# The first column group of x0: from a transposing load to two row loads and TensorE transposes

## The chip, the cores and the metric

The kernel runs on one core of one Trainium2 chip. The metric is the device time of one execution in microseconds (us); lower is better. Before the change it is 133.1 us, the median of three runs (133.09, 133.1 and 134.2).

The engines are named as in the profile: PE is TensorE (PEld its weight loads), DVE is VectorE, ACT is ScalarE, POOL is GpSimd, SP is SyncE. SPq and ACTq are the DMA queues that SP and ACT issue on.

## The reference

Six cross layers over a batch of 4096 rows with 416 features, all in bfloat16:

```python
B, F, D, L = 4096, 26, 16, 6
Din = min(F * D, 1024)          # 416
# x0: (B, Din), ws: (L, Din, Din), bs: (L, Din), all bfloat16
x = x0
for l in range(L):
    x = x0 * (x @ ws[l] + bs[l]) + x
return x
```

## The kernel before

**Layout.** In the first five layers x is held transposed: features on the partitions, batch rows along the columns. The 416 features are three blocks of 128 (the tiles `XM`, one column block k for each) and a remainder of 32 (the tiles `XR`). The batch is cut into two super-blocks s of 2048 columns, each into four groups g0 to g3 of 512. `XM[0]` holds x0 transposed. The remainder of the four groups of one s is stacked on the 128 partitions of `XR[0]`; `XRd` holds the same with the halves swapped. `ident` is an identity matrix for transposes on PE.

**Loads.** `load_x0t(s, g)` (L74) brings 512 rows of x0, the first 384 features, transposed by the DMA into `XM[0]`: 384 KiB each, eight of them, all issued by SP. `load_wm(eng, l)` (L71) brings the main rows of layer l's weights (312 KiB), `load_wr0` (L87) the last 32 rows of layer 0's weights, four times, into `WR`. `load_xrem0` (L78) brings the remainder of x0 for s = 0 in four pieces of 64-byte segments into `xrig`, `load_xrem1` (L83) that of s = 1. `bsb` gets the biases. The order of the issues is the order of the program on each queue (L99 to L120): on SP the transposing loads of s = 0's g0 to g3, s = 1's g0, `xrem`, s = 1's g1 to g3, then the weights of later layers; on ACT the weights of layer 0, the biases, the four pieces of `xrig`, `WR`, and then one activation (L105), ahead of which the activation table is loaded. In this text T0 to T7 are the eight transposing loads in the order in which SP issues them, and WM0 and WR0 are the loads of layer 0's weights.

**PE before the data.** `pe_filler(8)` (L130) runs eight matmuls on constants. `bias_setup` (L137) transposes the biases on PE, and DVE copies them to `bM` and `bR`.

**First layer.** `first_layer(s)` (L197) takes two groups at a time (h = 0: g0, g1; h = 1: g2, g3). `full(m, gl)` (L202) accumulates three matmuls (k = 0 to 2) for output block m of one group. For s = 0, h = 0 the order is all of g0, then `x0_rem(0, ...)` (L146), which transposes the four pieces of `xrig` on PE and has DVE copy them to `XR[0]` and `XRd`, then all of g1. After that come the matmuls over the remainder rows (L223), which need `WR`, `XR[0]` and `XRd`. Then h = 1 does the same with g2 and g3, in the order m outer, group inner, and the matmuls of the remainder outputs (`mm_rem`). `ew_main` (L153) is the rest of a layer for one output block: ACT adds the bias out of PSUM, DVE multiplies by x0 and adds x.

**PSUM.** One pool of four buffers, each of two banks, serves all tiles of PE's output in turn (`tag="ps"`); a tile waits until the buffer that it takes is free.

**Afterwards.** Layers 1 to 4 are loops over (s, m) with PE, ACT and DVE overlapped; the last layer computes rows again and stores them.

Of the kernel before, what the change touches and what calls it, by code (L numbers as in the profile page):

```python
# [9 lines left out]
ACT = mybir.ActivationFunctionType  # L10
ALU = mybir.AluOpType
BF16 = mybir.dt.bfloat16
FP32 = mybir.dt.float32
# [3 lines left out]
def kernel(  # L17
# [7 lines left out]
    nc = tc.nc  # L25
    B, D = x0.shape
    L = ws.shape[0]
    P = 128
    NK = 3
    R = D - NK * P  # L30
    assert R == 32 and B == 4096 and D == 416 and L >= 2
    NS = 2
    NG = 4
    CW = 512
# [5 lines left out]
    big = ctx.enter_context(tc.tile_pool(name="big", bufs=1))  # L40
    tpool = ctx.enter_context(tc.tile_pool(name="tpool", bufs=4))
    opool = ctx.enter_context(tc.tile_pool(name="opool", bufs=10))
    psum = ctx.enter_context(tc.tile_pool(name="psum", bufs=4, space=bass.MemoryType.PSUM))

    x0_v = x0.rearrange("(bt p) d -> p bt d", p=P)
    out_v = out.rearrange("(bt p) d -> p bt d", p=P)

    ident = const.tile([P, P], BF16)
    dz = const.tile([P, 2], FP32)
    warm = const.tile([P, CW], BF16)  # L50
# [6 lines left out]
    bM = const.tile([P, NK, L], FP32)  # L57
    bR = const.tile([P, L], FP32)
    X0rows = big.tile([P, NBT, D], BF16)
    XLrows = big.tile([P, NBT, D], BF16)  # L60
    scrR = [big.tile([P, 4, P], BF16, name=f"scrR{s}") for s in range(NS)]
    xrem = big.tile([P, 16, R], BF16)
    xrig = big.tile([P, NS, 4, P], BF16)
    XRd = big.tile([P, NS * CW], BF16)
    XM = [big.tile([P, NK, B], BF16, name=f"XM{i}") for i in range(3)]
    XR = [big.tile([P, NS * CW], BF16, name=f"XR{i}") for i in range(3)]

    def col0(s, g):
        return SW * s + CW * g

    def load_wm(eng, l):  # L71
        eng.dma_start(WM[:, l], ws[l, 0:NK * P, :].rearrange("(k p) n -> p k n", p=P))

    def load_x0t(s, g):  # L74
        c0 = col0(s, g)
        nc.sync.dma_start_transpose(out=XM[0][:, :, c0:c0 + CW], in_=x0[c0:c0 + CW, 0:NK * P])  # L76

    def load_xrem0():  # L78
        with nc.allow_non_contiguous_dma(reason="64B row segments"):
            for i in range(4):  # L80
                nc.scalar.dma_start(xrig[:, 0, i, :].rearrange("p (g r) -> p g r", g=NG), x0_v[:, i:16:4, NK * P:D])

    def load_xrem1():  # L83
        with nc.allow_non_contiguous_dma(reason="64B row segments"):
# [2 lines left out]
    def load_wr0():  # L87
        nc.scalar.dma_start(WR[:, 0, :], ws[0:1, NK * P:D, :].broadcast_to([NG, R, D]))
# [7 lines left out]
    nc.gpsimd.memset(ones[:], 1.0)  # L96
    nc.gpsimd.memset(WD[:], 0.0)

    load_x0t(0, 0)  # L99
    load_wm(nc.scalar, 0)  # L100
    nc.scalar.dma_start(bsb[:], bs[:, :])
    load_x0t(0, 1)
    load_xrem0()
    load_wr0()
    nc.scalar.activation(dz[:, 1:2], dz[:, 0:1], ACT.Identity, bias=dz[:, 0:1], scale=1.0)  # L105
    for g in range(2, NG):
        load_x0t(0, g)
    load_x0t(1, 0)
# [13 lines left out]
    def fill_wd(l0, l1):  # L122
        for g in range(NG):
            nc.gpsimd.tensor_copy(WD[32 * g:32 * g + 32, l0:l1, g, :], WR[32 * g:32 * g + 32, l0:l1, NK * P:D])  # L124

    fill_wd(0, 1)
    nc.gpsimd.tensor_copy(xrig[:, 1].rearrange("p i (g r) -> p i g r", g=NG), xrem[:].rearrange("p (g i) r -> p i g r", g=NG))
    fill_wd(1, L)

    def pe_filler(n):  # L130
        wps = psum.tile([P, CW], FP32, tag="ps", name="wps")
        for i in range(n):
            nc.tensor.matmul(wps[:], lhsT=warm[:, 0:P], rhs=warm[:], start=(i == 0), stop=(i == n - 1))  # L133

    pe_filler(8)

    def bias_setup():  # L137
        pb = psum.tile([P, 4, 8], BF16, tag="ps", name="pb")
        for m in range(NK):
            nc.tensor.transpose(pb[:, m, 0:L], bsb[0:L, 128 * m:128 * m + 128], ident[0:L, 0:L])  # L140
        for g in range(NG):
            nc.tensor.transpose(pb[32 * g:32 * g + 32, 3, 0:L], bsb[0:L, NK * P:D], ident[0:L, 0:L], tile_position=(0, 32 * g))
        nc.vector.tensor_copy(bM[:], pb[:, 0:NK, 0:L])
        nc.vector.tensor_copy(bR[:], pb[:, 3, 0:L])

    def x0_rem(s, tpr):  # L146
        for i in range(4):
            nc.tensor.transpose(tpr[:, 128 * i:128 * i + 128], xrig[:, s, i, :], ident[:])
        for dst, src in ((slice(0, P), slice(0, P)), (slice(64, P), slice(0, 64)), (slice(0, 64), slice(64, P))):
            to = XR[0] if dst == src else XRd  # L150
            nc.vector.tensor_copy(to[dst, CW * s:CW * s + CW], tpr[src])

    def ew_main(l, s, m, h, pt, cur, nxt):  # L153
        c0 = col0(s, 2 * h)
        t = tpool.tile([P, 2 * CW], BF16, name="t")
        nc.scalar.activation(t[:], pt[:].rearrange("p a b -> p (a b)"), ACT.Identity, bias=bM[:, m, l:l + 1], scale=1.0)  # L156
        nc.vector.tensor_tensor(out=t[:], in0=t[:], in1=XM[0][:, m, c0:c0 + 2 * CW], op=ALU.mult)  # L157
        nc.vector.tensor_tensor(out=nxt[:, m, c0:c0 + 2 * CW], in0=t[:], in1=cur[:, m, c0:c0 + 2 * CW], op=ALU.add)  # L158

    def ew_rem(l, s, pr, curR, nxtR):  # L160
        tr = tpool.tile([P, 2 * CW], BF16, name="t")
        nc.scalar.activation(tr[:, 0:CW], pr, ACT.Identity, bias=bR[:, l:l + 1], scale=1.0)  # L162
        nc.vector.tensor_tensor(out=tr[:, 0:CW], in0=tr[:, 0:CW], in1=XR[0][:, CW * s:CW * s + CW], op=ALU.mult)
        nc.vector.tensor_tensor(out=nxtR[:, CW * s:CW * s + CW], in0=tr[:, 0:CW], in1=curR[:, CW * s:CW * s + CW], op=ALU.add)  # L164
# [15 lines left out]
    def mm_rem(l, s, pr, cur, curR):  # L180
        for g in range(NG):
            nc.tensor.matmul(pr[32 * g:32 * g + 32, :], lhsT=WD[:, l, g, :], rhs=curR[:, CW * s:CW * s + CW],  # L182
                             start=True, stop=False, tile_position=(0, 32 * g))
        for k in range(NK):
            for g in range(NG):
                c0 = col0(s, g)
                nc.tensor.matmul(pr[32 * g:32 * g + 32, :], lhsT=WM[:, l, k, NK * P:D], rhs=cur[:, k, c0:c0 + CW],  # L187
                      start=False, stop=(k == NK - 1), tile_position=(0, 32 * g))
# [8 lines left out]
    def first_layer(s):  # L197
        cur, curR, nxt, nxtR = XM[0], XR[0], XM[1], XR[1]
        for h in range(2):
            pt = [psum.tile([P, 2, CW], FP32, tag="ps", name=f"ph{m}") for m in range(NK)]  # L200

            def full(m, gl):  # L202
                c0 = col0(s, 2 * h + gl)
                for k in range(NK):
                    nc.tensor.matmul(pt[m][:, gl, :], lhsT=WM[:, 0, k, 128 * m:128 * m + 128], rhs=cur[:, k, c0:c0 + CW],  # L205
                                     start=(k == 0), stop=False)

            if s == 0 and h == 0:
                for gl in range(2):
                    for m in range(NK):  # L210
                        full(m, gl)
                    if gl == 0:
                        tp0 = psum.tile([P, CW], BF16, tag="ps", name="tpr")
                        x0_rem(0, tp0[:])
            else:
                for m in range(NK):
                    for gl in range(2):
                        full(m, gl)
            for m in range(NK):
                for gl in range(2):  # L220
                    rg = 32 * ((2 * h + gl) ^ (2 if m == 1 else 0))
                    src = XRd if m == 1 else curR
                    nc.tensor.matmul(pt[m][:, gl, :], lhsT=WR[rg:rg + 32, 0, 128 * m:128 * m + 128],  # L223
                                     rhs=src[rg:rg + 32, CW * s:CW * s + CW],
                                     start=False, stop=True, tile_position=(rg, 0))
            if h == 1:
                pr = psum.tile([P, 2, CW], FP32, tag="ps", name="pr")
                mm_rem(0, s, pr[:, 0, :], cur, curR)
                if s == 0:
                    x0_rem(1, pr[:, 1, :].bitcast(BF16)[:, 0:CW])  # L230
            for m in range(NK):
                ew_main(0, s, m, h, pt[m], cur, nxt)
            if h == 1:
                ew_rem(0, s, pr[:, 0, :], curR, nxtR)

    bias_setup()
    for s in range(NS):
        first_layer(s)

# [41 lines left out]
    l = LL  # L281
# [98 lines left out]
```

## Time and profile before

| what | us |
|---|---|
| median of three runs | 133.1 |
| the profiled execution, own time | 133.1 |
| its span, first to last instruction | 131.2 |
| PE busy | 122.8 (94%) |
| DVE busy | 108.2 (83%) |
| ACT busy | 83.0 (63%) |
| POOL busy | 7.6 (6%) |
| the eight transposing loads, issue to landing, least / median / most | 4.8 / 5.6 / 6.5 |

The mean granted clock of TensorE is 0.998 of full speed. A busy PE is not a PE at its peak: matmuls are pipelined, and one of 512 columns is listed with 0.38 us while the next starts earlier. The DMA share of a core is the mean over its 16 DMA engines.

```profile
L76 SPq DMA_TRANSPOSE XM<-in_x_dram x8: 1378/2044/2574, 0.7 to 16.1; - x8
DMA to landing us min/median/max: 4.8/5.6/6.5
```

These two lines are from the instructions that touch the tile XM: SP spends 1.4 to 2.6 us on the issue of each transposing load (the numbers are ns, least, median and most, then the first and last start in us), and each lands 4.8 to 6.5 us after its issue began.

### The profile page before, as it was taken

The numbers are of one execution on the slowest core, as the hardware profiler recorded it, in microseconds if no ns is written. First come the engines' busy times: TensorE is split into PE (matmuls) and PEld (weight loads), VectorE is DVE, ScalarE is ACT, GpSimd is POOL, SyncE is SP. The second block draws the span as 40 slices with busy tenths as digits, with TensorE's granted clock in tenths as the row PEclk, the third lists the DMA queues.
The fourth block names the chain that finished last, engine by engine and source line by source line (L and its number), as shares of the span: only waits on it lengthen the run. The fifth ranks groups of instructions, "written<-read, shape, count | busy, mean of one in ns | idle before, by whom it ended". The sixth has DMA issues, their size and how long they took to land.

```text
span 131.2 us, 3924 instructions
## 1 busy us (share of the span) xinstructions
PE 122.8 (94%) x1687; PEld 54.5 (42%) x1687; DVE 108.2 (83%) x184; ACT 83.0 (63%) x89; POOL 7.6 (6%) x19
## 2 busy tenths in 40 slices
PE   5889999999999999999999999999999999999920
PEld 2333343344444344545444444434444454554400
DVE  1033989999989898989898989898989999988990
ACT  0035485598858668857759666849574975484740
POOL 4002200800000000000000000000002200000000
PEclk9999999999999999999999999999999999999999
DMA  3999999999980000000000000000599999956453
GB/s 100 245 208 228 158 158 275 265 329 332 335 242 3 5 2 5 0 0 5 0 5 0 5 0 5 0 5 0 104 117 196 188 185 208 272 175 197 166 181 110
DMA packets 42089, 16.45 MB, mean 125 GB/s; under 512 B 30798, under 2 KB 42072, under 8 KB 42072
## 3 DMA queue, kind: packets, MB, share of 16 engines
q1 hardware_dynamic: 39272, 15.53, 54.0%
q10 hardware_dynamic: 2800, 0.67, 2.6%
q8 instruction: 13, 0.21, 0.7%
q14 instruction: 4, 0.03, 0.1%
HBM read 6.23 MB, written 3.41 MB: 74 GB/s over the span
## 4 chain that ended last, share of the span: by engine, by line
PE 82%; SPq 5%; DMA 4%; DVE 3%; issue 2%; ACT 1%; DVEq 0%
PE pt L170 49%; PE pt L294 10%; PE ph L205 9%; PE pt L176 5%; PE pr L187 5%; SPq L76 5%; DMA XM<-in_x_dram 4%; DVE t L313 2%; PE pr L182 2%; PE ph L223 1%; PE pt L300 1%; PE pt L303 1%; ACT t L312 1%; DVE o L314 1%; DVE t L323 0%
## 5 line engine op out<-in xcount | busy, mean ns | idle before, releaser
L170 PE MATMUL pt<-XM,WM 128*32 128x512 bf16 x1152 | 65.2, 379 | 0.0
L156 ACT ACTIVATE t<-pt,bM 128x1024 bf16<-128x1024 f32 x48 | 49.5, 1114 | 19.1 <-PE pt L176 19.1
L157 DVE TENSOR_TENSOR t<-t,XM 128x1024 bf16<-128x1024 bf16 x60 | 41.7, 697 | 5.7 <-ACT t L156 5.7
L158 DVE TENSOR_TENSOR XM<-t,XM 128x1024 bf16<-128x1024 bf16 x60 | 41.9, 700 | 3.4
L170 PEld LDWEIGHTS <-WM 128*32 128x32 bf16 x1152 | 29.8, 97 | 33.9 <-issue 5.4
L294 PE MATMUL pt<-WM,XM 128*128 128x416 bf16 x96 | 17.7, 340 | 0.0
L156 ACT ACTIVATE t<-ph,bM 128x1024 bf16<-128x1024 f32 x12 | 12.5, 1111 | 7.4 <-PE ph L223 7.4
L205 PE MATMUL ph<-XM,WM 128*128 128x512 bf16 x72 | 16.5, 379 | 0.7 <-DMA XM<-in_x_dram 0.6
L312 ACT CAST t<-pt 128x832 bf16<-128x832 f32 x15 | 12.2, 854 | 7.2 <-PE pt L303 5.2
L294 PEld LDWEIGHTS <-XM 128*128 128x128 bf16 x96 | 9.0, 98 | 8.4 <-issue 1.7
L205 PEld LDWEIGHTS <-WM 128*128 128x128 bf16 x72 | 6.8, 98 | 9.1 <-issue 1.8
L313 DVE TENSOR_TENSOR t<-t,X0rows 128x832 bf16<-128x832 bf16 x15 | 8.8, 586 | 0.9 <-ACT t L312 0.9
L314 DVE TENSOR_TENSOR o<-t,XLrows 128x832 bf16<-128x832 bf16 x15 | 8.9, 592 | 0.6
L162 ACT ACTIVATE t<-pr,bR 128x512 bf16<-128x512 f32 x10 | 6.4, 685 | 3.0 <-PE pr L187 2.1
L187 PE MATMUL pr<-XM,WM 128*32 128x512 bf16 x120 | 8.2, 379 | 0.0
L176 PE MATMUL pt<-XR,WR 32*128 32x512 bf16 x96 | 7.3, 379 | 0.0
L248 POOL COPY XLrows<-scrR 128x512 bf16<-128x512 bf16 x2 | 1.7, 878 | 74.8 <-DMA scrR<-XR 74.8
L105 ACT ACT_TABLE_LOAD x1 | 1.3, 1283 | 6.3 <-DMA XM<-in_x_dram 6.3
L164 DVE TENSOR_TENSOR XR<-t,XR 128x512 bf16<-128x512 bf16 x10 | 4.2, 425 | 0.7
L133 PE MATMUL wps<-warm 128*128 128x512 bf16 x8 | 3.3, 594 | 1.5 <-DVE dz L94 1.5
L187 PEld LDWEIGHTS <-WM 128*32 128x32 bf16 x120 | 3.2, 97 | 3.0
L124 POOL COPY WD<-WR 32x32 bf16<-32x32 bf16 (+1 forms) x8 | 3.4, 430 | 16.2 <-DMA WR<-in_ws_dram 15.8
(40 smaller groups left out, 34.3 us busy)
## 6 DMA issues: line engine op xcount, KB each, us to landing
X0rows<-in_x_dram SPq DMA_DIRECT2D x4, 832.0 KB, 11.6
out_dram<-o SPq DMA_DIRECT2D x15, 208.0 KB, 2.5
WM<-in_ws_dram SPq DMA_DIRECT2D x5, 312.0 KB
WR<-in_ws_dram SPq DMA_DIRECT2D x4, 130.0 KB, 4.1
WM<-in_ws_dram ACTq DMA_DIRECT2D x1, 312.0 KB
XM<-in_x_dram SPq DMA_TRANSPOSE x8, 5.6
xrig<-in_x_dram ACTq DMA_DIRECT2D x4, 32.0 KB, 4.1
xrem<-in_x_dram SPq DMA_DIRECT2D x1, 128.0 KB, 3.8
```

The costliest lines, as they stand in the source:

```text
L76: nc.sync.dma_start_transpose(out=XM[0][:, :, c0:c0 + CW], in_=x0[c0:c0 + CW, 0:NK * P])
L156: nc.scalar.activation(t[:], pt[:].rearrange("p a b -> p (a b)"), ACT.Identity, bias=bM[:, m, l:l + 1], scale=1.0)
L157: nc.vector.tensor_tensor(out=t[:], in0=t[:], in1=XM[0][:, m, c0:c0 + 2 * CW], op=ALU.mult)
L158: nc.vector.tensor_tensor(out=nxt[:, m, c0:c0 + 2 * CW], in0=t[:], in1=cur[:, m, c0:c0 + 2 * CW], op=ALU.add)
L170: nc.tensor.matmul(pts[g // 2][32 * q:32 * q + 32, g % 2, :], lhsT=WM[:, l, k, 128 * m + 32 * q:128 * m + 32 * q + 32], rhs=cur[:, k, c0:c ...
L176: nc.tensor.matmul(pts[g // 2][:, g % 2, :], lhsT=WR[32 * g:32 * g + 32, l, 128 * m:128 * m + 128], rhs=curR[32 * g:32 * g + 32, CW * s:CW ...
L187: nc.tensor.matmul(pr[32 * g:32 * g + 32, :], lhsT=WM[:, l, k, NK * P:D], rhs=cur[:, k, c0:c0 + CW], start=False, stop=(k == NK - 1), tile ...
L205: nc.tensor.matmul(pt[m][:, gl, :], lhsT=WM[:, 0, k, 128 * m:128 * m + 128], rhs=cur[:, k, c0:c0 + CW], start=(k == 0), stop=False)
L294: nc.tensor.matmul(py[g // 2][:, g % 2, 0:D], lhsT=cur[:, k, q_cols(q, g)], rhs=WM[:, l, k, :], start=((not rem_first) and k == 0), stop=( ...
L312: nc.scalar.copy(tv, py[h][:, :, 0:D])
L313: nc.vector.tensor_tensor(out=tv, in0=tv, in1=X0rows[:, b0:b0 + 5:4, :], op=ALU.mult)
L314: nc.vector.tensor_tensor(out=o[:], in0=tv, in1=XLrows[:, b0:b0 + 5:4, :], op=ALU.add)
```

## The change

For s = 0's g0 there is no transposing load any more. Its 512 rows come as rows, in two loads of two 128-row tiles each (`xg0`, 208 KiB each, all 416 features), on ACT's queue; WM0 moves from ACT's queue to the head of SP's. PE transposes the 12 blocks of 128 by 128 into one PSUM tile `tg0`, and DVE copies them to `XM[0]` in three pieces. g0's remainder comes out of the same rows: POOL copies it to `xrig`, and the four loads of `xrig` bring the other three groups alone. The activation that brings the table load moves up between the second and the third of them. Of the fillers five run ahead of the first six transposes and two behind them; the bias transposes follow, and then the other six. The bias lies in the same PSUM buffer as the fillers. The matmuls of g0 take k in the outer loop for the first two output blocks; the third block follows whole.

```diff
+    xg0 = [big.tile([P, 2, D], BF16, name=f"xg0{a}") for a in range(2)]
...
-    def load_xrem0():
+    def load_xrem0(i0, i1):
         with nc.allow_non_contiguous_dma(reason="64B row segments"):
-            for i in range(4):
-                nc.scalar.dma_start(xrig[:, 0, i, :].rearrange("p (g r) -> p g r", g=NG), x0_v[:, i:16:4, NK * P:D])
+            for i in range(i0, i1):
+                nc.scalar.dma_start(xrig[:, 0, i, R:P].rearrange("p (g r) -> p g r", g=NG - 1),
+                                    x0_v[:, i + 4:16:4, NK * P:D])
...
-    load_x0t(0, 0)
-    load_wm(nc.scalar, 0)
+    nc.scalar.dma_start(xg0[0][:], x0_v[:, 0:2, :])
+    load_wm(nc.sync, 0)
     nc.scalar.dma_start(bsb[:], bs[:, :])
+    nc.scalar.dma_start(xg0[1][:], x0_v[:, 2:4, :])
     load_x0t(0, 1)
-    load_xrem0()
+    load_xrem0(0, 2)
+    tc.keep_in_program_order(nc.scalar.activation(dz[:, 1:2], dz[:, 0:1], ACT.Identity, bias=dz[:, 0:1], scale=1.0))
+    load_xrem0(2, 4)
     load_wr0()
-    nc.scalar.activation(dz[:, 1:2], dz[:, 0:1], ACT.Identity, bias=dz[:, 0:1], scale=1.0)
...
+    for a in range(2):
+        nc.gpsimd.tensor_copy(xrig[:, 0, 2 * a:2 * a + 2, 0:R], xg0[a][:, :, NK * P:D])
     fill_wd(0, 1)
...
+    wps = psum.tile([P, 2, CW], FP32, tag="ps", name="wps")
+    tg0 = psum.tile([P, NK, CW], BF16, tag="ps", name="tg0")
+    pb = wps[:, 1, :].bitcast(BF16)[:, 0:32].rearrange("p (m l) -> p m l", m=4)
...
+    def g0_transposes(a):
+        for k in range(NK):
+            for i in range(2):
+                c = 128 * (2 * a + i)
+                nc.tensor.transpose(tg0[:, k, c:c + 128], xg0[a][:, i, 128 * k:128 * k + 128], ident[:])
...
-    pe_filler(8)
+    pe_filler(5)
+    g0_transposes(0)
+    pe_filler(2)
+    bias_transposes()
+    g0_transposes(1)
+    for k in range(NK):
+        nc.vector.tensor_copy(XM[0][:, k, 0:CW], tg0[:, k, :])
+    nc.vector.tensor_copy(bM[:], pb[:, 0:NK, 0:L])
+    nc.vector.tensor_copy(bR[:], pb[:, 3, 0:L])
...
             if s == 0 and h == 0:
-                for gl in range(2):
-                    for m in range(NK):
-                        full(m, gl)
-                    if gl == 0:
-                        tp0 = psum.tile([P, CW], BF16, tag="ps", name="tpr")
-                        x0_rem(0, tp0[:])
+                for k in range(NK):
+                    for m in range(NK - 1):
+                        full(m, 0, (k,))
+                full(NK - 1, 0)
+                tp0 = psum.tile([P, CW], BF16, tag="ps", name="tpr")
+                x0_rem(0, tp0[:])
+                for m in range(NK):
+                    full(m, 1)
```

## The prediction

> **What bounds the kernel now.** I read the page first. TensorE (PE) is busy 94% of a 131.2 us span and 82% of the chain that ended last. The rest of the chain that bears on this change stands at its start, so I then asked for the chain of waits of the first 30 us. Columns: start us, us, what.
>
> ```profile
> span 131.2 us, 3924 instructions
> PE 82%; SPq 5%; DMA 4%; DVE 3%; issue 2%; ACT 1%; DVEq 0%
> 0.73 1.38 SPq L76
> 2.16 2.57 SPq L76
> 4.79 2.09 SPq L76
> 6.92 5.25 DMA XM<-in_x_dram
> 12.21 3.40 PE ph L205 x15
> ```
>
> SP issues the transposing loads T0, T1, T2, T3 (groups g0 to g3) one after another. T3 is issued at 6.92 and lands 5.25 us later; at 12.21 PE starts the first matmul that reads it, and from there the chain is PE without a gap to 120 us. So I call 12.21 the junction J: the end moves by what J moves. Next the timeline up to J (start, us, engine, line, operation, count, idle before it).
>
> ```profile
> 1.45 3.34 PE L133 MATMUL wps<-warm 128*128 128x512 bf16 x8 [1.45 <-DVE dz L94]
> 4.73 0.22 PE L140 MATMUL pb<-ident,bsb 6*128 6x6 bf16 x3
> 5.63 2.10 PE L205 MATMUL ph<-XM,WM 128*128 128x512 bf16 x9 [0.56 <-DMA XM<-in_x_dram]
> 8.26 0.48 PE L148 MATMUL tpr<-ident,xrig 128*128 128x128 bf16 x2 [0.42 <-DMA xrig<-in_x_dram]
> 8.73 2.10 PE L205 MATMUL ph<-XM,WM 128*128 128x512 bf16 x9
> 8.78 0.42 DVE L151 COPY XR<-tpr 128x512 bf16<-128x512 bf16 x1 [3.42 <-PE tpr L148]
> 10.76 0.39 PE L223 MATMUL ph<-XR,WR 32*128 32x512 bf16 x2
> 11.30 3.02 PE L205 MATMUL ph<-XM,WM 128*128 128x512 bf16 x12
> ```
>
> Two more pieces of the chain of waits give prices.
>
> ```profile
> 17.12 0.33 PE pr L148 x4
> 17.45 3.88 PE ph L205 x18
> ```
>
> A 512-column matmul costs 3.88/18 = 0.216 us, a 128-column transpose 0.33/4 = 0.083. PE's work from its first real matmul to J is 9 matmuls (1.94), four transposes (0.33), 9 matmuls (1.94), the row matmuls (10.76 to 11.30, 0.54) and 3 matmuls (0.65): 5.40 us. It takes 12.21 - 5.63 = 6.58. So PE stalls 1.2 us: 0.82 around the xrig transposes (7.57 to 8.73 for 0.33 of work), 0.09 before L223, 0.26 for T3. The change can gain those stalls; it can lose by starting later than 5.63.
>
> **Order of the DMAs.** Times of packets and landings here are the trace's records of them. WM0 was issued at 0.73, its data passed 1.82 to 3.45, it landed at 3.96. T0: data 2.98 to 4.83, landed 5.59. bsb, issued 1.19 while T0 was being issued (0.73 to 2.11), passed at 3.8, amid T0. The first xrig piece, issued 1.91 to 2.30, began at 4.69, at T0's end; the other three ran mixed with T1 (4.84 to 7.17), the last landing at 8.47. WR0, issued 5.61, behind T2's start (4.79), passed 9.05 to 10.16, after T2 (7.18 to 9.06). I read from this that a load of either queue is served roughly where it was issued among the transposes. A lone transpose moves 57 KiB in 0.2 us, so 384 KiB in 1.35 us; plain 832-byte rows reach 70 KiB in 0.2 us.
>
> **The change, part by part.**
>
> *SP.* T0's issue (1.38) goes, WM0's (0.43 on ACT) comes: T1 is issued at about 1.2 instead of 2.16. All later transposes move up.
>
> *ACT's queue.* xg0 half 0 (0.43, as WM0), bsb (0.69), xg0 half 1 from 1.9 to 2.3, two xrig pieces to about 3.5, the activation, two more pieces, WR0. The table load and its activation (1.28 + 0.29) leave 6.28 to 7.87, where nothing waited, for about 3.5; ACT is first needed at 11.19, so that costs nothing on ACT itself. Whether the DMA issues behind them wait for them no row shows. If not, the last xrig piece is issued by 4.6; if so, by 6.1. WR0 and the last xrig piece also wait for an earlier DMA to land (in the trace xrig's fourth issue starts at 3.98 after WM0's landing at 3.96, WR0's at 5.61 after T0's at 5.59); the loads they would now wait for land by 5.4, so this holds back at most WR0.
>
> *The first row load.* Halves of 208 KiB each. WM0 and half 0 pass together. If the two queues double the slow start (94 KiB by 2.6), half 0's share is through at 3.1, else at 3.5; with 0.5 to land (WM0's) 3.6 to 4.0. I take 3.8. The five fillers end at 1.45 + 5 x 0.43 = 3.6 (weight loads of L133 stand 0.43 apart), so PE is idle 0.2 us.
>
> *PE until the second half.* Six transposes: 0.50 at 0.083, 1.0 at half that rate; I take 0.7, to 4.5, as the clock rose about there before. Two fillers at 0.22 to 0.43: 0.6, to 5.1. The bias transposes took 4.73 to 5.06: 0.33, to 5.4.
>
> *The second row load.* Issued 1.9 to 2.3, in the second half of T1's issue (1.2 to 2.6), so its data falls in the second half of T1's, which has to follow the 520 KiB ahead (through at 3.5): 4.2 to 4.9. Plus 0.5: lands at 5.4. Bounds: 4.8 if it passes T1, 6.8 if T1 goes wholly first.
>
> *To the first matmul.* Six more transposes 0.50 (5.9), DVE's copy of one 128x512 block 0.42 (the L151 row) and two hand-offs of 0.05: matmuls start at s = 6.4. That is 0.8 later than before. The other two copies cost nothing: 0.42 each beside two matmuls of 0.43, which is what the k-outer order is for; the column block left for last waits for the bias copies (0.18 + 0.16), done when PE gets there. DVE was idle from 5.37 to 8.78, GpSimd from 2.1 to 10.85, so the added copies there are free.
>
> *From s to J.* 5.40 + 0.05 pacing = 5.45, plus stalls that stay. xrig is needed at s + 2.0 = 8.4; issued by 4.6, its pieces run with T2 and land near 8.1; held by the table load, 8.6 to 9.1. Stall 0 to 0.7; I take 0.05, since the smaller pieces (96 columns of remainder instead of 128) take less time. WR0, needed at 10.7, is issued 5.4 to 6.7, lands 9.5 to 10.6: 0, bound 0.4. T3: data ended at 11.48 from T0's start at 2.98, that is 8.5 us of which four transposes are 5.4 and 3.1 is xrig, WR0 and stalls. Now three transposes (4.05), the second row load (0.6) and 2.0 to 2.5 of the rest start at 3.5: done 10.2 to 10.7, landed 0.6 later, 10.8 to 11.3. PE comes at J, so T3 stops deciding.
>
> Sum: J = 6.4 + 5.45 + 0.05 = 11.9 against 12.21, a gain of 0.3 us. The profiled execution's own time is 133.1 with 1.9 outside its span, equal to the median 133.1: forecast 132.8. Its own range: s from 6.1 to 6.8 and stalls to 0.3 give 132.5 to 133.5.
>
> Behind J the covers hold: s=1's groups T5 (landed 17.10, read from 17.94) and T6, T7 move up with SP by more than PE does.
>
> **Rivals.**
>
> *1. PE stays at half clock (slower).* Filler and first matmuls ran at 0.43 spacing, L205's at 0.216, after PE had been busy without a break from 1.45 to 4.79. Now it is idle before xg0 half 0 and again before half 1, and does transposes between. If full rate is not granted by about 5.9, six transposes cost 0.5 more and the 9 matmuls 9 x 0.21 = 1.9 more: J = 11.9 + 2.4 = 14.3, time 135.2; if it comes in the middle of them, 134.2 or so. For: the unbroken run is gone. Against: rate changed once only, and seven of eight fillers stay. Chance 0.20. The Trainium skill, page "TensorE: Matmul & The Clock Gate", Part 4, says that a transpose does not count as PE-busy in the way a matmul does and that the full clock does not engage for it; by its 275 ns each the 12 would take 3.3 us against 1.0 by the L148 row, and J would be near 14.0 (an estimate from that page). The L148 row (0.083 each at a granted clock of 1.00) speaks against the price, but its transposes stand among matmuls; no row here shows transposes after an idle PE.
>
> *2. The second row load waits for all of T1 (slower, mostly inside 1%).* As WR0 did behind T2. T1's data ends near 5.5, the load then shares with T2 until 6.3, lands at 6.8: s = 7.8, J = 13.3, time 134.2; with xrig and WR0 pushed back too, 134.6. For: WR0's row. Against: bsb amid T0. Chance 0.17.
>
> *3. Everything early (faster).* Half 0's data is through at 3.0 and lands 0.4 later (WM0's first queue did so), half 1 follows it directly and lands by 4.5, and at full rate a transpose is a quarter of a matmul (0.054): 3.4 + 0.33 + 0.43 + 0.33 = 4.5 for PE, the second six to 4.8, s = 5.35, J = 10.8: 131.7. T3 must then also land before 10.8, without the stall that its data showed from 9.4 to 10.2; with T3 at 11.1 it is 132.0. For: both loads head their queues. Against: SP's T1 is issued before half 1. Chance 0.23, of which 0.18 past 1%.
>
> *4. The load behind the table load (xrig at 9.1):* J = 12.6, 133.5; counted with the forecast, whose chance is 0.40.
>
> **Numbers.** 1% is 1.33 us, about what a measurement of this kernel can tell from no change (its three runs spread over 1.1). Over 1% faster: 0.18 of rival 3, and 0.02 for a gain not seen. Over 1% slower: rival 1 but for 0.03, and 0.06 of rival 2: 0.23. Within: 0.57. Range: from rival 3 at 131.6 to rival 2's end and rival 1's middle at 134.7; it leaves out rival 1's upper half (0.1) and about 0.1 of tails.
>
> **What would show it.** T1's issue near 1.2; first matmul on g0 at 6.4 (rivals: 5.35, 7.8); its nine matmuls 0.216 apart (rival 1: 0.43); no PE idle before the xrig transposes; PE, not a DMA, ahead of J in the chain, with T3 landed before 11.4. I am wrong if the end moves by other than J, or if a transposing load still ends the front.

## The result, and the profile after

The changed kernel takes 138.21 us (median of six runs, 136.93 to 138.83) against 133.23 for the kernel before on the same chip. The ratio is 1.035, 95% interval 1.031 to 1.039: slower. Forecast were 132.8 and at most 134.7. The profiled execution took 138.66, with a span of 136.6 (before 131.2). The ratios leave out executions more than 1.5% above the fastest of their kernel, the medians do not, and the profiled executions of three experiments (rows first with WR0 on SP, and both under "One remainder load instead of four") are among those left out.

The page of the changed kernel, the span and the shares of the chain that ended last:

```profile
span 136.6 us, 3953 instructions
PE 85%; DMA 5%; DVE 4%; issue 2%; ACTq 1%; ACT 1%; DVEq 0%
```

SPq, 5% of the chain before, is gone from it: the transposing loads no longer set the front. The changed kernel's chain of waits near its start (start us, us, what):

```profile
1.92 7.12 DMA xg<-in_x_dram
9.04 0.05 issue
9.09 0.83 PE tg L148 x6
9.93 0.02 issue
9.95 0.44 DVE XM L162
10.39 0.04 issue
10.43 3.79 PE ph L225 x9
14.22 0.22 PE tpr L168 x4
14.44 1.94 PE ph L225 x9
16.39 0.54 PE ph L245 x6
16.92 3.99 PE ph L225 x18
```

Two lines hold nearly the whole loss. The second row load is issued at 1.92, just behind the biases, and takes 7.12 us, so that the first matmul on g0 starts at s = 10.43 and not at 5.63 as before. And the nine matmuls that follow take 3.79, which is 0.42 each, where the next nine take 1.94: PE is still at half its clock (a 512-column matmul took 0.216 at the full clock in the kernel before). Three of the 18 matmuls at 16.92 come before the first one on g3, so J = 16.92 + 0.65 = 17.57; it was 12.21. The sum of the parts: +4.80 for the later start (s, the start of the first matmul on g0), +1.85 for the half clock, -1.17 for PE's stalls of before, which are gone, and -0.11 for faster xrig transposes, together +5.37. J moved by 5.36 and the span by 5.4.

The timeline of the changed kernel shows how PE got there (start, us, engine, line, operation, count, idle before it):

```profile
1.46 3.17 PE L142 MATMUL wps<-warm 128*128 128x512 bf16 x7 [1.46 <-DVE dz L96]
...
5.67 0.82 PE L148 MATMUL tg<-ident,xg 128*128 128x128 bf16 x6 [1.04 <-DMA xg<-in_x_dram]
...
9.06 0.63 ACTq L90 DMA_DIRECT2D WR<-in_ws_dram  x1
9.09 0.82 PE L148 MATMUL tg<-ident,xg 128*128 128x128 bf16 x6 [2.32 <-DMA xg<-in_x_dram]
```

All seven fillers run in one piece to 4.63: the two that stand behind the first six transposes in the program were scheduled ahead of them. Then PE is idle 1.04 us for the first row load and 2.32 for the second. The trace's clock record grants the full clock at 13.88; before it was 4.41. The record starts with that grant, so the mean granted clock of 0.998 given for the kernel before leaves out the half clock ahead of it. The line of ACT's queue is a further reading: WR0 is issued at 9.06, right behind the landing of the second row load at 9.04. The first transposing loads themselves became slower: T1 and T2 took 8.2 and 8.1 us from issue to landing and T3 6.6, where the eight of before took 4.8 to 6.5; the later four took 4.6 to 5.9.

### The profile page after: what moved, and what is told of

It reads as the page before. It is cut to its first block, busy times and chain, and to the rows that moved or that the text cites. A ratio compares the mean times of both kernels' runs of the same rounds, so it can differ in the third digit from the quotient of the medians.

```text
span 136.6 us, 3953 instructions
## 1 busy us (share of the span) xinstructions
PE 125.3 (92%) x1698; PEld 55.9 (41%) x1698; DVE 109.3 (80%) x187; ACT 83.0 (61%) x89; POOL 8.9 (7%) x21
## 3 DMA queue, kind: packets, MB, share of 16 engines
HBM read 6.63 MB, written 3.41 MB: 73 GB/s over the span
## 4 chain that ended last, share of the span: by engine, by line
PE 85%; DMA 5%; DVE 4%; issue 2%; ACTq 1%; ACT 1%; DVEq 0%
PE pt L190 47%; PE ph L225 13%; PE pt L315 10%; DMA xg<-in_x_dram 5%; PE pt L196 5%; PE pr L207 5%; DVE t L334 2%; PE pr L202 2%; PE ph L245 2%; PE pt L321 1%; PE pt L324 1%; ACT t L333 1%; PE tg L148 1%; DVE o L335 0%; ACTq L103 0%
## 5 line engine op out<-in xcount | busy, mean ns | idle before, releaser
L178 DVE TENSOR_TENSOR XM<-t,XM 128x1024 bf16<-128x1024 bf16 x60 | 41.4, 692 | 3.4
L190 PEld LDWEIGHTS <-WM 128*32 128x32 bf16 x1152 | 29.8, 97 | 33.9 <-issue 5.4
L225 PE MATMUL ph<-XM,WM 128*128 128x512 bf16 x72 | 18.1, 407 | 0.5 <-DVE XM L162 0.5
L128 POOL COPY WD<-WR 32x32 bf16<-32x32 bf16 (+1 forms) x8 | 4.9, 611 | 11.7 <-DMA WR<-in_ws_dram 11.4
L148 PE MATMUL tg<-ident,xg 128*128 128x128 bf16 x12 | 1.6, 308 | 3.4 <-DMA xg<-in_x_dram 3.4
```

What stands on the lines that cost most here:

```text
L190: nc.tensor.matmul(pts[g // 2][32 * q:32 * q + 32, g % 2, :], lhsT=WM[:, l, k, 128 * m + 32 * q:128 * m + 32 * q + 32], rhs=cur[:, k, c0:c ...
```

## The experiments

**My theory** after the result: the second row load is late through its place in the order of the issues, behind T1 and the biases, so that its packets pass beside T1's, both slowly; the half clock follows from PE's two gaps. **Rivals:** the load is slow through its source (both row loads and T1 read x0); it waits wholly behind T1, and the sharing costs nothing of its own; the clock is a loss apart from the late load and not its consequence.

### The row loads ahead of the biases

```diff
-    nc.scalar.dma_start(bsb[:], bs[:, :])
     nc.scalar.dma_start(xg0[1][:], x0_v[:, 2:4, :])
+    nc.scalar.dma_start(bsb[:], bs[:, :])
```

> The second row load moves ahead of the biases on ACT's queue, so it is issued at about 1.26 us, with T1 and not behind its first half. If the order of issue alone put it behind T1 (order theory), it lands by 5.6, the matmuls on g0 start by 6.7 and the time is 133 to 135 us. If it is the mixing of plain rows on one queue with transposes on the other that slows both (mixing theory), it still passes beside T1: it lands at 7 or later, the matmuls start after 8.3 and the time stays at 136 or more.

Measured: 135.92, ratio 1.022 (1.015 to 1.030); the profiled execution took 134.48, the least of the four (up to 136.89), span 132.4. Its timeline and its chain of waits:

```profile
5.00 0.80 PE L148 MATMUL tg<-ident,xg 128*128 128x128 bf16 x6 [0.38 <-DMA xg<-in_x_dram]
...
7.55 2.10 PE L225 MATMUL ph<-XM,WM 128*128 128x512 bf16 x9 [0.52 <-DVE XM L162]
```

```profile
1.81 4.40 DMA bsb<-in_bs_dram
6.21 0.02 issue
6.24 5.85 DMA WR<-in_ws_dram
12.09 0.05 issue
12.13 0.60 PE ph L245 x6
```

The swap moves the issue by 0.65 us (1.27 instead of 1.92) and the landing by 3.6 (5.40 instead of 9.04). PE's gap in front of the transposes shrinks to 0.38, the full clock is there from 5.64 and nine matmuls take 2.10 with the last one's drain. That supports the order of the issues. All six runs in which the row load stands ahead of the biases or of T1 have it landed between 5.29 and 5.72; the three with it in its old place (one of them, below, reads other rows) between 7.49 and 9.04. But a new wait comes to the end of the chain: WR0 is issued at 6.24, 0.02 behind the landing of the biases, lands at 12.09, and PE waits for it with the remainder rows. The front was ended by one load and is now ended by the next.

### The second row load on SP, ahead of T1

```diff
-    nc.scalar.dma_start(xg0[1][:], x0_v[:, 2:4, :])
+    nc.sync.dma_start(xg0[1][:], x0_v[:, 2:4, :])
     load_x0t(0, 1)
```

> The second row load goes to SP's queue, behind WM0 and ahead of T1, so no transpose is issued before it. Order and mixing theories both expect it to land at 4.8 to 5.4, the matmuls on g0 to start near 6.2 and a time of 132.8 to 134.5, the upper end if the clock is still at half then. If the row reads themselves are slow in this place (third theory), it lands after 7 and the time stays above 136.

Measured: 135.92, ratio 1.020 (1.013 to 1.027), span 134.6. The load lands at 5.72. The chain of waits:

```profile
7.57 4.00 PE ph L225 x9
```

The start is that of the run before (7.57 against 7.55), but the nine matmuls take 4.00: the full clock comes at 12.88 only. So the order matters on the other queue as well, and an early load alone does not bring the clock. PE is idle no longer here than there ahead of 7.0 (0.57 us in front of the first transposes here; 0.38 and 0.46 in front of the transposes and of the biases there).

### More filler: the clock alone

```diff
-    pe_filler(5)
+    pe_filler(20)
```

> Fifteen more fillers keep PE busy while the second row load is on its way, nothing else moves. Clock theory: the row load still lands near 9, but the nine matmuls on g0 then run 0.216 apart instead of 0.42, about 2 us less: 136.2 to 137.0 against 138.2. If the half clock cost nothing that the loads would not have cost anyway, the time stays within 0.4 us of 138.2.

Measured: 136.92, ratio 1.025 (1.019 to 1.032), profiled 136.83, span 134.7. The chain of waits:

```profile
1.45 7.27 PE wps L142 x22
8.73 0.34 PE tg L148 x6
...
9.33 0.46 PE tg L148 x6
...
10.29 1.89 PE ph L225 x8
...
15.09 3.99 PE ph L225 x18
```

The fillers keep PE busy to 8.73, the full clock is granted at 6.25, and s is 10.29, close to the changed kernel's 10.43. Now J is 15.09 + 0.65 = 15.74 against 17.57, and the profiled time is lower by the same 1.83 us (the medians by 1.29). Of this 0.14 is the earlier start, which the fillers set here; the other 1.69 is the clock's share by itself, near the forecast's price for rival 1 without the transposes (9 x 0.21 = 1.9). The second row load, untouched here, landed at 7.82 and not at 9.04: this landing varies by more than a microsecond between executions.

### An extra load of the same size in the kernel before

```diff
+    dum = big.tile([P, 2, D], BF16, name="dum")
...
     nc.scalar.dma_start(bsb[:], bs[:, :])
+    nc.scalar.dma_start(dum[:], ws[5, 0:2 * P, :].rearrange("(k p) n -> p k n", p=P))
```

> The kernel before, with one more load of 208 KiB of plain rows (of the last layer's weights, read by nobody) on ACT's queue behind the biases, where the second row load stands. Order theory: the load costs its own passage, 0.6 to 0.8 us, so T3 lands near 12.9 and the time is 133.8 to 134.2. Mixing theory: it passes beside T1 and both crawl; it takes over 5 us from issue to landing, T1's data takes at least 1.5 us longer than the 2.3 us of before, and the time is 134.5 or more.

Measured, in one execution: 135.78 beside a median of 133.04, span 133.6. The dummy, issued at 1.92, passed between T0 and T1, from about 4.5 to 6.0 at up to 136 KiB per 0.5 us, and landed at 6.57: the slow passage beside a transposing load was not seen, a miss. It is slower all the same. The chain of waits:

```profile
2.18 6.94 DMA XM<-in_x_dram
9.11 0.02 issue
9.13 4.17 DMA WR<-in_ws_dram
```

WR0 is issued at 9.13, 0.02 behind the landing of T1; in the kernel before it was 5.61, 0.02 behind the landing of T0. One load more in front of it, and WR0 waits for the next landing in the row. The trace's record of this issue shows a wait for a semaphore, the one that T1's landing raises; eight semaphores serve all the loads in turn, so a load goes out only once the eighth before it has landed.

The same dummy with its rows out of x0 was meant to tell whether the source matters:

```diff
+    nc.scalar.dma_start(dum[:], x0_v[:, 2:4, :])
```

> As the kernel before with the unread 208 KiB load, but from x0's own rows in place of the weights. With the weights it passed between T0 and T1 (4.5 to 6.0) and landed at 6.56. Source theory: the data passes slower, lands after 7.5, and T1's landing moves from 9.1 to 10 or later. Otherwise the same within 0.4 us. In both, WR0 waits for T1's landing, since the added load shifts by one which earlier load it waits for, so the time stays at 135.5 or more.

Measured, in one execution: 135.56, span 133.5, landing 6.68 (6.57 from the weights), WR0 at 9.28. The source makes no difference here.

### The second row load out of the weights

```diff
-    nc.scalar.dma_start(xg0[1][:], x0_v[:, 2:4, :])
+    nc.scalar.dma_start(xg0[1][:], ws[5, 0:2 * P, :].rearrange("(k p) n -> p k n", p=P))
```

> The kernel after, but the second row load reads 208 KiB of rows of the last layer's weights in place of x0's rows; size, place and queue stay, and half of g0 holds other values. If the slow passage comes from reading the same tensor that T1 reads (source theory), it lands by 6.0, data of both moves at 100 KiB or more in half a microsecond, and the time falls to 134.5 to 136. If any plain rows beside a transpose on the other queue are slow (mixing theory), it lands at 7.8 to 9 as with x0's rows and the time stays at 136.9 to 138.8.

Half of g0 then holds other values. Measured: 137.47, ratio 1.031 (1.025 to 1.037), profiled 136.84, span 134.7. The chain of waits:

```profile
1.94 5.55 DMA xg<-in_ws_dram
...
8.56 3.76 PE ph L225 x9
```

The load landed at 7.49, where the same load out of x0 landed at 9.04 and, with more filler, at 7.82. That is 0.33 below the lower of the two, which differ by 1.22 themselves, and later than the 6.0 that was expected if the source were the cause: that both loads read x0 does not explain the lateness. The full clock was granted at 5.42 here, taken back at 8.84 and granted again at 12.25, so the nine matmuls ran nearly all at half of it.

### The second row load wholly behind T1

```diff
-    nc.scalar.dma_start(xg0[1][:], x0_v[:, 2:4, :])
     load_x0t(0, 1)
+    nc.sync.dma_start(xg0[1][:], x0_v[:, 2:4, :])
```

> The second row load stands on SP's queue wholly behind T1 and ahead of T2. Order theory: it lands later than in the kernel after or as late (9 us or more), since all of T1 goes first. Mixing theory: one queue serves one after the other, T1's data takes 1.4 to 2.0 us, the row load then 0.7 to 1.0, and it lands at 6.3 to 7.5, earlier than the 7.8 to 9.0 of the two profiles in which it passed beside T1.

Measured, in one execution: 137.89, span 136.0. T1's data passed from 3.7 to 5.8 and the row load's from 5.8 to 7.0; it landed at 7.62, close above what was expected. The chain of waits:

```profile
9.00 4.00 PE ph L225 x9
```

Issued at 2.87 behind T1 on one queue it lands no later than at 1.92 amid T1 on the other (9.04, 7.82): a late place costs about what a mixed place costs. On this queue, where no biases stand between, the place ahead of T1 gave 5.72 and the place behind it 7.62; what the biases add on ACT's queue was not run by itself. With s = 9.00 and half clock the time is near that of the changed kernel.

### First attempts at a mend, which missed

*Rows, then WR0, then the biases.* Since WR0 was late in the first experiment, I moved it ahead of the biases, behind the rows, and let the second six transposes go before the bias transposes, with two fillers more.

```diff
+    nc.scalar.dma_start(xg0[1][:], x0_v[:, 2:4, :])
+    load_wr0()
     nc.scalar.dma_start(bsb[:], bs[:, :])
-    nc.scalar.dma_start(xg0[1][:], x0_v[:, 2:4, :])
...
-    load_wr0()
...
-    pe_filler(5)
+    pe_filler(7)
...
+    g0_transposes(1)
     bias_transposes()
-    g0_transposes(1)
```

> Both row loads head ACT's queue, WR0 follows them, the biases after that, two more fillers, and the second six transposes no longer stand behind the bias transposes. If order and clock are the whole loss, the row load lands at 5.4 or before, the matmuls on g0 start by 6.7 at full clock, WR0 no longer ends anything, and the time is 132.7 to 133.6, level with the kernel before. If the time stays at 134.5 or more, a third cost is left in the change.

Measured: 137.69, ratio 1.033 (1.027 to 1.039). The row load landed at 5.38 and all 12 transposes were done by 6.74. The timeline:

```profile
9.10 0.23 PE L152 MATMUL wps<-ident,bsb 6*128 6x6 bf16 x3 [2.36 <-DMA bsb<-in_bs_dram]
```

The biases, 4.9 KB, now landed at 9.06, behind WR0, whose rows passed beside the transposing loads, at 26 to 73 KiB per 0.5 us in all from 6.5 to 8.5. PE had 2.36 us of idle. The full clock, granted at 6.59, was taken back from 10.01 to 13.42, and the nine matmuls took 3.37. The lateness moved to the load behind the row loads and WR0.

*The kernel before with WR0 on SP between T2 and T3,* to see whether one queue keeps them apart.

```diff
-        nc.scalar.dma_start(WR[:, 0, :], ws[0:1, NK * P:D, :].broadcast_to([NG, R, D]))
+        nc.sync.dma_start(WR[:, 0, :], ws[0:1, NK * P:D, :].broadcast_to([NG, R, D]))
...
-    load_wr0()
...
-    for g in range(2, NG):
-        load_x0t(0, g)
+    load_x0t(0, 2)
+    load_wr0()
+    load_x0t(0, 3)
```

> The kernel before with nothing of the change, but WR0 moved from ACT's queue to SP's, between T2 and T3, so that it no longer passes beside a transpose. Mixing theory: T2's or T3's data shows no stall like that of 9.4 to 10.2, T3 lands near 11.3 and not 12.1, and the time falls by 0.3 to 0.7 us. If a stall of a transpose has nothing to do with the plain rows beside it, T3 lands at 12.1 or, with WR0 ahead of it, 12.4, and the time is the same or 0.3 longer.

Measured: 133.1, ratio 0.999 (0.995 to 1.002): no change. T3 is issued at 7.57, lands at 12.25, and PE still waits for it; WR0's packets mix with T3's at 70 to 90 KiB per 0.5 us on the same queue. I had expected one queue to keep them apart; it does not.

### Rows first, and WR0 on SP between T2 and T3

The biases stand behind the second row load again, WR0 goes from ACT's queue to SP's, and the second six transposes stand ahead of the bias transposes.

```diff
-        nc.scalar.dma_start(WR[:, 0, :], ws[0:1, NK * P:D, :].broadcast_to([NG, R, D]))
+        nc.sync.dma_start(WR[:, 0, :], ws[0:1, NK * P:D, :].broadcast_to([NG, R, D]))
...
-    nc.scalar.dma_start(bsb[:], bs[:, :])
     nc.scalar.dma_start(xg0[1][:], x0_v[:, 2:4, :])
+    nc.scalar.dma_start(bsb[:], bs[:, :])
...
-    load_wr0()
...
-    for g in range(2, NG):
-        load_x0t(0, g)
+    load_x0t(0, 2)
+    load_wr0()
+    load_x0t(0, 3)
...
-    pe_filler(5)
+    pe_filler(7)
...
+    g0_transposes(1)
     bias_transposes()
-    g0_transposes(1)
```

> The kernel after with both row loads at the head of ACT's queue and the biases behind them, WR0 on SP's queue between T2 and T3, two more fillers, and the second six transposes ahead of the bias transposes. If order, mixing and clock are the whole loss, the second row load lands by 5.4, the matmuls on g0 start at 6.5 to 7.0 at full clock, WR0 lands before 10 and PE has no stall behind it: 12.0 to 12.6 for the first matmul on g3, 133.0 to 133.7 us. If it stays at 134.5 or more, a cost is left that these three do not explain.

Measured: 136.98, ratio 1.020 (1.013 to 1.026). The first matmul on g0 starts at 6.89 with the full clock, near the forecast's 6.4. The chain of waits:

```profile
1.25 6.36 DMA XM<-in_x_dram
7.61 0.02 issue
7.63 4.38 DMA xrig<-in_x_dram
12.01 0.05 issue
12.05 0.23 PE tpr L168
12.28 3.36 PE ph L225 x9
```

With the front mended, the limit on loads in flight ends it: the last xrig piece waits for the landing of T1 (7.61), lands at 12.01, and PE is idle 1.14 and 1.60 us in front of its transposes. In this execution, which took 137.97 and was the longest of the six (least 135.52), the clock also falls back from 12.65 to 16.06, and the nine matmuls on g1 take 3.36; whether it did in the shorter ones is not known.

### One remainder load instead of four

Fewer loads means fewer that wait. The remainder of g1 to g3 comes in one load, and POOL copies it into the four places of xrig; WR0 stands behind it on ACT, as it issues there again. The rest is as in the run before. The lines of these loads, against the changed kernel:

```diff
-                nc.scalar.dma_start(xrig[:, 0, i, R:P].rearrange("p (g r) -> p g r", g=NG - 1),
-                                    x0_v[:, i + 4:16:4, NK * P:D])
+            nc.scalar.dma_start(xrem0[:], x0_v[:, 4:16, NK * P:D])
...
-    load_xrem0(0, 2)
+    load_xrem0()
+    load_wr0()
...
-    load_xrem0(2, 4)
-    load_wr0()
...
+    nc.gpsimd.tensor_copy(xrig[:, 0, :, R:P].rearrange("p i (g r) -> p i g r", g=NG - 1), xrem0[:].rearrange("p (g i) r -> p i g r", g=NG - 1))
```

> The kernel after with both row loads at the head of ACT's queue, the biases behind them, the remainder of g1 to g3 in one load (POOL copies it to xrig) in place of four, WR0 right behind it, two more fillers and the second six transposes ahead of the bias transposes. Queue theory (a load beyond the eighth is issued only when an earlier one has landed): nothing in front of T3 waits for a landing any more, no xrig or WR0 stall is left on PE, the matmuls on g0 start at 6.5 to 7.0 and the first matmul on g3 comes at 12.0 to 12.7: 132.9 to 133.8 us. If PE still waits for a remainder or WR0 that was issued at once, the plain rows beside transposes are the cost and the time stays at 134.5 or more.

Measured: 135.54, ratio 1.012 (1.006 to 1.018); the profiled execution took 136.21. The chain of waits:

```profile
2.46 7.90 DMA xrem<-in_x_dram
...
11.59 3.19 PE ph L224 x8
```

s is 6.55, but the remainder load, issued at 2.46, took 7.90 us, its rows and WR0's passing beside T2; PE was idle 2.31 and the clock fell at 11.01. As a control, the kernel before with a single remainder load of all four groups and POOL's copy:

```diff
-                nc.scalar.dma_start(xrig[:, 0, i, :].rearrange("p (g r) -> p g r", g=NG), x0_v[:, i:16:4, NK * P:D])
+            nc.scalar.dma_start(xrem0[:], x0_v[:, 0:16, NK * P:D])
...
+    nc.gpsimd.tensor_copy(xrig[:, 0].rearrange("p i (g r) -> p i g r", g=NG), xrem0[:].rearrange("p (g i) r -> p i g r", g=NG))
```

> The kernel before with nothing of the change, but the remainder of s = 0 in one load that POOL copies to xrig, in place of four loads. Queue theory: WR0 is issued near 3 in place of 5.6 and no load ahead of T3 waits for a landing; PE's stall of 0.8 at the xrig transposes changes only with the landing of T1 (8.7), so the front ends at T3 as before: 132.6 to 133.2. If the POOL copy comes late, it ends the stall instead: 133.3 to 134.0.

Measured: 133.22, ratio 0.998 (0.994 to 1.001): the single load is neither gain nor loss of time by itself, though a shorter end of the span (told with the last variant) may hide a small loss at the front.

### All of it together

The kernel of one remainder load, with WR0 on SP between T2 and T3 (the lines that differ from it):

```diff
-        nc.scalar.dma_start(WR[:, 0, :], ws[0:1, NK * P:D, :].broadcast_to([NG, R, D]))
+        nc.sync.dma_start(WR[:, 0, :], ws[0:1, NK * P:D, :].broadcast_to([NG, R, D]))
...
     load_xrem0()
-    load_wr0()
...
-    for g in range(2, NG):
-        load_x0t(0, g)
+    load_x0t(0, 2)
+    load_wr0()
+    load_x0t(0, 3)
```

> The last version with WR0 on SP's queue between T2 and T3, so that no plain rows pass beside T1 and T2 and still no load ahead of T3 waits for a landing. If WR0's rows beside T2 were the loss, the remainder lands by 8.5, PE waits less than 0.5 us for it, the first matmul on g3 comes at 12.0 to 12.8 and the time is 133.0 to 133.9. If the 64-byte remainder load is slow beside transposes by itself, it lands after 9.5, PE stalls 1 us or more at the xrig transposes and the time stays at 134.5 or more.

Measured: 134.04 (median of 12), ratio 1.0036 (0.9999 to 1.0073); profiled 133.5, span 131.7. The chain of waits:

```profile
2.46 6.89 DMA xrem<-in_x_dram
9.35 0.05 issue
9.40 0.52 POOL xrig L130
9.91 0.05 issue
9.96 0.40 PE tpr L167 x4
10.36 1.94 PE ph L224 x9
12.30 0.54 PE ph L244 x6
12.83 3.99 PE ph L224 x18
```

s is 6.47, the clock full from 4.78, and J = 12.83 + 0.65 = 13.48. The remainder load landed at 9.35 (I had expected 8.5 at the latest), and PE waited 1.39 us for it:

```profile
9.96 0.40 PE L167 MATMUL tpr<-ident,xrig 128*128 128x128 bf16 x4 [1.39 <-POOL xrig L130]
```

J is still 1.27 us later than in the kernel before, and so, by 1.22, is DVE's last multiplication or addition. The span grew by only 0.5, because its end behind that instruction is shorter: 2.65 us instead of 3.31. All three profiles with one remainder load have this end (2.65 to 2.71) and the twelve others do not (3.31 to 3.41), so it goes with the smaller number of loads and not with the new front. So with the late row load and the half clock gone and fewer loads held back by landings, the change comes out within about 0.7% of the kernel before (the medians of all executions are 134.04 and 133.07), with 0.7 us won at the end of the span in which the new front has no part, and no variant that I ran beats it.

## Why the prediction was wrong, step by step

**The step that failed first is "The second row load": landing at 5.4, bounds 4.8 and 6.8.** It landed at 9.04, and with more filler at 7.82, outside both bounds. I had taken the slowest case to be all of T1 ahead of it at T1's own rate. What the trace shows is both passing together from 4.5 to 8.5 at 50 to 107 KiB per 0.5 us in all, against 140 for a transposing load alone and 180 for plain rows alone. T1's data took from 3.6 to 7.5, 3.9 us instead of 2.3 before. The term for sharing was a sum of bytes at full rates; the runs put a loss of rate in its place. With the load issued 0.65 us sooner it lands at 5.40, which is the forecast's own number. Of the start's miss, 10.43 against 6.4, this landing is 3.6 us and the second six transposes at half clock are 0.33 (0.83 against 0.50).

**"The first row load: 3.6 to 4.0"** was 5.62 in the changed kernel. WM0, which passes together with it, landed at 4.91, before at 3.96. The rate of two queues at their start was estimated from one: the row load's data were through by about 4.5 (estimate 3.1 to 3.5), and it landed 1.1 behind them instead of 0.5.

**"PE until the second half": two fillers behind the first six transposes.** They ran ahead of them, so nothing covered the gap. With the row load at 9.04 they could not have covered it anyway.

**The clock.** Rival 1 came true, with its price: 1.85 us measured in the changed kernel, 1.69 by the run with more filler. My mistake was to treat rivals 1 and 2 as exclusive, 0.20 and 0.17. In the changed kernel the late loads left PE idle, and the full clock did not come. The two can also come apart: with more filler the load was late (7.82) and the clock full, and with the row load on SP the load was early (5.72) and the clock half. Together they reach J = 17.57, past both of the rivals' ends. The transposes cost 0.83/6 = 0.14 us each at half clock and 0.057 to 0.077 in the run with more filler. The Trainium skill, page "TensorE: Matmul & The Clock Gate", Part 4, gives 275 ns, about twice the first; the measurement decides. Its other half, that the full clock does not engage for transposes, does not hold here as it stands: the full clock was granted while the transposes ran, at 5.64 with the rows first and at 6.59 with WR0 behind the rows, and with more filler they ran at it.

**The queue of loads.** The prediction saw that WR0 and an xrig piece wait for earlier landings and priced it at nothing ("holds back at most WR0"). The loads that they waited for did not land by 5.4: the last xrig piece went out behind the biases (6.07), WR0 behind the second row load (9.04). In the changed kernel this cost nothing all the same, as WR0 landed at 13.5 and was needed at 16.4. Once the row load is on time it is the next bound: 2.74 us of idle PE in the profile of rows first with WR0 on SP, and 2.7 us of time (135.78 against 133.04, one execution; 2.4 by the spans) with one unread load added to the kernel before, its own passage included.

**What was right.** T1 was issued at 1.23 (forecast 1.2). The end moved with J, 5.36 and 5.4. The first of DVE's three copies is on the chain with 0.44 (forecast 0.42); the other two, POOL's two (0.24 each) and the early table load (3.43 to 4.72 on ACT) cost nothing that the chain shows. The stalls of 1.17 us in front of J did go, and T3, landed at 13.7, waits for PE and not PE for it, though the step "landed 10.8 to 11.3" was off by 2.4 us or more. The forecast's s = 6.4 at full clock was reached by the two variants with rows first and one remainder load (6.55, 6.47), but not its 5.45 from s to J: there the remainder landed at 10.36 and 9.35, against the forecast's 8.1 to 9.1.

**Open.** Why plain rows and transposing loads lose rate beside each other: neither the source (the weights instead of x0) nor the queue (WR0 on SP) removes it, and I have no run that shows the mechanism. It was also not always there: the dummy in the kernel before passed between T0 and T1 at up to 136 KiB per 0.5 us. WR0 may be a case of its own: its semaphore, in the changed kernel, has one update 1.1 us after the issue and four more at the landing (13.44 to 13.49), where each row load has sixteen. That fits a load that four of the 16 DMA engines carry alone; no run spread it over more. The clock's share differs between executions, as the two early-load runs show; how much of the spread of 136.93 to 138.83 comes from that was not measured.

## What to carry to other kernels

The place of a load in the order of all loads, over both queues, can be worth more than its size: a load issued 0.65 us sooner landed 2.4 to 3.6 us earlier, and a load that nobody reads cost 2.7 us. When a front is rebuilt, list the loads in order of issue, mark which landing each one has to wait for, and put what PE needs first ahead of everything else, the small transfers too. And price a late load and the half clock that can follow from the idle PE together, not as two alternatives; where the load cannot come sooner, filler can still win the clock (1.69 us here).

## What the runs showed of the hardware

**Loads in flight.** Issues followed a landing within 0.02 to 0.03 us in each case: 9.06 after 9.04 in the changed kernel, 6.24 after 6.21 with the rows first, 9.13 after 9.11 with the dummy, 7.63 after 7.61 with WR0 on SP. Each of these issues waits, in its trace record, for the semaphore that the earlier load raises (number 106 for WR0 and the second row load in the changed kernel), and eight numbers serve all loads of both queues. So the limit of eight loads in flight stands in the program's waits; no run shows one of the chip.

**Clock.** In the clock records the full clock lasts 3.41, 6.83, 116.05, 119.47, 122.88 or 126.29 us, and a break between two stretches of it 3.41: 1, 2, 34, 35, 36, 37 and 1 times 3.413. It changes only at such steps, and their phase differs between executions. The Trainium skill, page "TensorE: Matmul & The Clock Gate", Part 1, says that the clock is decided by free-running windows of 3413 ns, and these records agree.

Counted back from the grant in such steps, PE was busy for 2.96 us of the step that ended with the grant in the kernel before, 3.03 with the rows first and 3.41 with more filler. With the row load on SP it was busy for 2.84 and 2.90 of two steps that ended without one (2.64 to 6.05, 6.05 to 9.46). So a small difference in how PE's work falls into the steps goes with grants as far apart as 5.64 and 12.88 in these two runs with an early row load; that the phase of the steps made the difference was not shown by a run of its own. A bound between 2.90 and 2.96 is no rule: with one remainder load the clock came after a step with 2.74, all filler. Once full, the clock outlasted a step with 2.02 us of PE in it (the last variant, an idle PE of 1.39 us) and was lost after steps with 1.27 (row load out of the weights, idle 1.63 and 0.52) and 1.06 (WR0 behind the rows, idle 2.36).
